# Two feed-forward layers in two phases over all tokens, the gated tiles kept in float32, each half weight tile decoded when it is needed, SBUF laid out by hand

## The chip, the core and the metric

The program runs on one core of one Trainium2 chip. The metric is the device time of one execution in microseconds (us); three executions of the kernel before are known, and one more execution, with the profiler on, gives the trace. TensorE (PE) multiplies; VectorE (DVE), ScalarE (ACT) and GpSimd (POOL) work elementwise; SyncE (SP) issues the transfers.

## The reference, cut to what matters

Clustered attention over 2 batches of 8 heads (768 positions of 64), whose output becomes 1536 tokens of 512, and then two feed-forward layers. Weights arrive as float64.

```
attn = softmax(where(same cluster, scale * q @ k.T, -1e9)) @ v
x = attn.transpose(0, 2, 1, 3).reshape(1536, 512)
h = np.maximum(x @ w_in, 0.0)                                # w_in 512 x 2048
x = (h * h @ w_out).astype(np.float32)                       # w_out 2048 x 512
h = x @ w_in2
g = h * (1.0 / (1.0 + np.exp(-1.702 * h)))
return (g @ w_out2).astype(np.float32)
```

## The kernel before, in words

**Products.** A float32 operand is split into a high part (a cast to float32r) and a low part (what the cast lost, one subtraction); a product is three passes, high by high, low by high, high by low.

**Attention.** Sixteen heads go in eight pairs, as 96 query tiles: `scores` (L470, L473), `peak` on DVE (L479), `exponents` on ACT (L487), transposes (L494) and their copies (L500), then `values` (L510), the ratio transposes (L527) and `whole` (L537), which multiplies by the ratio and writes a quarter of a token chunk `xs`. The order of everything is a table of keys: each piece is put `at` a number that counts query tiles, the list is sorted, and each engine gets its instructions in that order.

**Feed-forward.** There are 4 token chunks of 384 tokens and 16 weight tiles m (128 hidden units each) in a layer. A step is one chunk with one weight tile, 64 steps a layer, chunk by chunk. In a step `hidden` runs 12 products of 128x384 (L597); the gate makes `r` on ACT (L610, and L616 square; in the second layer L612 sigmoid and L618 product on DVE), its high part `gh` by an ACT cast (L622) and its low part `gl` on DVE (L626). LAG = 3 steps later `reduce_out` runs the output products: 12 of 128x384 in the first layer (L645), 9 of 128x512 in the second (L651), which add up in PSUM over all m. `leave` copies a finished chunk out (L660, L662, or L670 with a transfer), and `split_x` splits the next chunk (L172, L173).

**Weights.** A weight tile has a half for `hidden` (w_in) and a half for the output products (w_out). Both halves come in one transfer of 1024 KB, as float64 bit patterns, and each is decoded in seven stages: magnitude on ACT (L136), clamp, shift and two joins on DVE (L139, L143, L147, L151), a cast on ACT (L157) and a subtraction on POOL (L161). All 16 weight tiles of a layer are held in SBUF for its whole length, so all 32 half tiles must have been decoded by the end of its first chunk: NMID = 5 weight tiles are decoded under the attention, the other 11 during the first chunk's 16 steps; all 16 of the second layer's during the first layer's last chunk and the second layer's first.

## Time and profile before

| what | value |
|---|---|
| three timed executions | 849.98, 848.15, 849.47 us, median 849.47 |
| profiled execution, span | 848.9 us; no other own time of it is known |
| busy in it | PE 807.3, DVE 503.6, ACT 444.0, POOL 231.5 us |
| attention's last product, first product of the feed-forward layers | up to 269.66 us, from 269.66 us |
| last product | ends at 845.36 us |

The profiled execution's own time is its span. The median of the timed runs is 0.6 us above it. Busy time is the sum of the durations of an engine's instructions; what an engine waited for is found in the chain of waits, which follows the work that ended last back from the end.

### The profile page before, as it was taken

Reading aid. Unit: us, or ns where it says so; the run is one execution under the profiler, and the core shown is the slowest. Engines: PE = TensorE matmul, PEld = TensorE weight load, DVE = VectorE, ACT = ScalarE, POOL = GpSimd, SP = SyncE. Lnnn points to the kernel's source line nnn. Section 1 sums busy time; section 2 is a strip of 40 time slices with the busy share of each in tenths; the row PEclk is TensorE's granted clock in tenths of the full one; section 3 lists DMA queues with packets and bytes.
Section 4 is the critical chain, followed back from the end, with each engine's and each line's share of the span. In section 5 each row is a group of like instructions: output and inputs, shape, how many; then the busy total and the mean of one; then the engine's idle time right before and its main releaser. Section 6 shows DMA issues by size and latency. Waiting matters only on the chain.

```text
span 848.9 us, 11910 instructions
## 1 busy us (share of the span) xinstructions
PE 807.3 (95%) x4509; PEld 683.5 (81%) x4509; DVE 503.6 (59%) x896; ACT 444.0 (52%) x890; POOL 231.5 (27%) x181
## 2 busy tenths in 40 slices
PE   6899999999999787999999999989879999999998
PEld 3766666666666787899999999979669999999997
DVE  6877777888889999611111228999983233232321
ACT  5787678788776655643443446564443233222221
POOL 5874474485303544300000003333330000000000
PEclk9899999999999989999999999999989999999999
DMA  4232233242131920000000025352111001000000
GB/s 131 75 103 51 71 85 105 73 128 66 29 149 58 390 97 3 1 1 1 1 1 1 1 78 207 141 195 76 52 48 38 1 1 38 0 1 8 31 1 37
DMA packets 13449, 54.60 MB, mean 64 GB/s; under 512 B 2192, under 2 KB 2192, under 8 KB 9296
## 3 DMA queue, kind: packets, MB, share of 16 engines
q1 hardware_dynamic: 13248, 53.45, 18.9%
q8 instruction: 35, 0.57, 0.3%
q10 hardware_dynamic: 144, 0.39, 0.1%
q14 instruction: 22, 0.18, 0.1%
HBM read 43.02 MB, written 3.15 MB: 54 GB/s over the span
## 4 chain that ended last, share of the span: by engine, by line
PE 68%; DVE 21%; issue 3%; ACT 2%; DMA 1%; POOL 1%; DVEq 0%; ACTq 0%
PE ps_h L597 21%; PE ps_y L651 13%; PE ps_y L645 9%; PE ps_p L494 8%; PE ps_v L510 8%; DVE w L147 5%; DVE w L139 4%; DVE w L151 4%; PE ps_s L470 3%; PE ps_s L473 3%; DVE gl L626 2%; DVE w L143 2%; PE ps_aff L333 1%; DVE r L618 1%; DVE unused L479 1%
## 5 line engine op out<-in xcount | busy, mean ns | idle before, releaser
L597 PE MATMUL ps_h<-xhl,w 128*128 128x384 f32 x1536 | 294.0, 339 | 8.4 <-ACT w L157 3.5
L597 PEld LDWEIGHTS ps_h<-xhl,w 128*128 128x128 f32 x1536 | 274.0, 190 | 17.1 <-ACT w L157 4.0
L161 POOL TENSOR_TENSOR w<-w,w 128x512 fp32r<-128x512 f32 x64 | 97.7, 1535 | 289.9 <-ACT w L157 271.9
L626 DVE TENSOR_TENSOR gl<-r,gh 128x384 fp32r<-128x384 f32 x128 | 77.2, 603 | 146.5 <-ACT gh L622 146.5
L645 PE MATMUL ps_y<-gh,w 128*128 128x384 f32 x512 | 131.9, 338 | 0.0
L651 PE MATMUL ps_y<-w,gh 128*128 128x512 f32 x384 | 121.0, 396 | 1.1 <-ACT gh L622 1.1
L494 PEld LDWEIGHTS ps_p<-ident,e 128*128 128x128 f32 x576 | 67.1, 142 | 56.0 <-ACT pt L500 23.3
L645 PE MATMUL ps_y<-gl,w 128*128 128x384 f32 x256 | 87.8, 343 | 14.1 <-DVE gl L626 14.1
L622 ACT CAST gh<-r 128x384 fp32r<-128x384 f32 x128 | 65.7, 514 | 64.9 <-DVE r L618 62.8
L494 PE MATMUL ps_p<-ident,e 128*128 128x128 f32 x576 | 99.2, 283 | 0.1
L479 DVE TENSOR_SCALAR_CACHE_REDUCE unused<-ps_s 128x768 bf16<-128x768 f32 x96 | 91.5, 953 | 11.4 <-PE ps_s L473 7.8
L487 ACT ACTIVATE e<-ps_s,nm 128x768 f32<-128x768 f32 x96 | 86.6, 902 | 21.9 <-DVE unused L479 13.9
L618 DVE TENSOR_TENSOR r<-ps_h,r 128x384 f32<-128x384 f32 x64 | 35.6, 556 | 104.3 <-ACT r L612 104.3
L645 PEld LDWEIGHTS ps_y<-gh,w 128*128 128x128 f32 x512 | 93.8, 191 | 0.3 <-ACT gh L622 0.3
L612 ACT ACTIVATE r<-ps_h 128x384 f32<-128x384 f32 x64 | 31.3, 490 | 103.6 <-PE ps_h L597 103.5
L651 PEld LDWEIGHTS ps_y<-w,gh 128*128 128x128 f32 x384 | 71.9, 190 | 13.7 <-ACT gh L622 1.7
L510 PE MATMUL ps_v<-pt,raw_v 128*64 128x384 f32 x384 | 82.3, 510 | 0.0
L651 PE MATMUL ps_y<-w,gl 128*128 128x512 f32 x192 | 77.0, 401 | 3.2 <-DVE gl L626 3.2
L500 DVE COPY pt<-ps_p 128x384 f32<-128x384 f32 x96 | 52.7, 549 | 34.3 <-PE ps_p L494 33.3
L610 ACT ACTIVATE r<-ps_h 128x384 f32<-128x384 f32 x64 | 31.2, 488 | 77.0 <-PE ps_h L597 77.0
L157 ACT CAST w<-w 128x512 fp32r<-128x512 f32 x64 | 39.6, 618 | 59.5 <-DVE w L151 59.4
L645 PEld LDWEIGHTS ps_y<-gl,w 128*128 128x128 f32 x256 | 48.9, 191 | 16.7 <-DVE gl L626 16.7
(102 smaller groups left out, 981.3 us busy)
## 6 DMA issues: line engine op xcount, KB each, us to landing
words<-in_w_dram SPq DMA_DIRECT2D x32, 1024.0 KB, 5.0
raw_k<-in_k_t_dram SPq DMA_DIRECT2D x8, 384.0 KB, 3.8
q<-x SPq DMA_DIRECT2D x16, 192.0 KB, 2.6
k<-k SPq DMA_DIRECT2D x16, 192.0 KB, 2.6
raw_v<-in_v_dram SPq DMA_DIRECT2D x8, 384.0 KB, 3.3
out_dram<-o SPq DMA_DIRECT2D x12, 256.0 KB, 2.1
raw_q<-in_q_t_dram SPq DMA_DIRECT2D x7, 384.0 KB, 3.5
q<-oht SPq DMA_DIRECT2D x14, 48.0 KB, 2.1
```

The costliest lines, as they stand in the source:

```text
L161: nc.gpsimd.tensor_tensor(out=t[:, 1, :], in0=x[i].bitcast(F32), in1=t[:, 0, :].bitcast(F32), op=ALU.subtract)
L479: nc.vector.tensor_scalar(out=unused, in0=s_t[g][:, :, :HALF], scalar1=-scale, scalar2=None, op0=ALU.mult, op1=ALU.min, accum_out=m_t[g])
L487: nc.scalar.activation(out=p_t[g].rearrange("p (n f) -> p n f", n=2), in_=s_t.pop(g)[:, :, :HALF], func=AF.Exp, bias=m_t.pop(g), scale=sca ...
L494: nc.tensor.transpose(ps[:, a * P:(a + 1) * P], p_t[g][:, t * P:(t + 1) * P], ident)
L500: (nc.vector.tensor_copy if u else nc.scalar.copy)(out=pt_t[n, j][:, u * TH:(u + 1) * TH, i * P:(i + 1) * P], in_=tp_t.pop((g, u))[:, :HAL ...
L510: nc.tensor.matmul(pv_t[n][j * D:(j + 1) * D, :HALF], lhsT=raw[n // 2, "v"][:, j, t, :], rhs=pt_t[n, j][:, t, :], start=(t == 0), stop=(t ...
L597: nc.tensor.matmul(ps[:, :HALF], lhsT=w[:, 0, a, kk * P:(kk + 1) * P], rhs=x[:, b, kk, :], start=(n == 0), stop=(n == 3 * KD - 1))
L618: nc.vector.tensor_tensor(out=t["r"], in0=t["ps"][:, :HALF], in1=t["r"], op=ALU.mult)
L622: nc.scalar.copy(out=t["gh"], in_=t["r"])
L626: nc.vector.tensor_tensor(out=gl, in0=t["r"], in1=t["gh"].bitcast(F32), op=ALU.subtract)
L645: nc.tensor.matmul(ps, lhsT=lh, rhs=rh, start=(m == 0 and e == 0), stop=(m == MF - 1 and e == 2))
L651: nc.tensor.matmul(ps, lhsT=lh, rhs=w[:, 1, a, :], start=(m == 0 and e == 0), stop=(m == MF - 1 and e == 2))
```

## The change

Each layer now runs in two phases over all 1536 tokens. In the hidden phase, 64 units (weight tile m by chunk c, m outermost) of 12 products each fill 16 tiles `g_t[m]` of gated values in float32, which stay in SBUF. In the output phase the chunks go in two groups g of two chunks s; for each m the output products of both chunks follow, in eight (second layer: six) PSUM banks. Just ahead of them `g_high` (ACT) and `g_low` (DVE) split one chunk's gated values into one of three places `ghl`.

w_in and w_out halves are now loaded (512 KB each, 64 transfers) and decoded apart, by a list of `jobs` that gives each half the unit at which its first stage stands, with 0.3 units between its stages and its load 2.7 units ahead. Decoded halves lie in a ring of two (w_in, and a few of w_out) or in places that have come free. Of the half tiles, 3 instead of 10 are decoded under the attention; 21 in the first hidden phase, 16 in the first output phase (8 of them the second layer's), 16 in the second hidden phase, 8 in the second output phase.

SBUF is two arenas of fixed size, one for float32r and one for float32, and every tile of it is a view at a written offset; the tile pools are gone. In PSUM the first eight units of the first layer use the attention's places, and the tile `banks` takes all eight banks at unit 8. `whole` now also splits its quarter of a chunk (a cast on ACT, a subtraction on DVE), and `split_x` and `xs` are gone; the first layer's results are split straight out of PSUM (`leave_high`, `leave_low`). LAST moves the last `values`, ratio and `whole` earlier, and everything is in one list of keys, in which the first four hidden units stand among the last `values`.

```diff
+LAST = dict(
+    values=(5.984, 6.484, 6.984, 7.484, 7.984, 8.484), inverse=4.238, spread=5.0, ratio=6.6, ratio_out=7.1, whole=8.9,
+)
...
-    LAG = 3 # steps from hidden to output products
-    W_EARLY = (51.456, 63.886) # query tiles at which the first weight tiles are decoded
-    W_PITCH = 4.887 # the next weight tiles: query tiles between them
-    W_FIRST = 0.265 # in steps: the rest of the first layer
...
+    KB = 1024
+    ROOM = {F32R: 97 * KB, F32: 110 * KB + 512}
+    arena = {t: arena_p.tile([P, n // 4], t, name=f"arena_{n}") for t, n in ROOM.items()}
...
+    xhl = [view(12 * KB * c, [2, KD, HALF], F32R) for c in range(NC)]
+    slots = [60 * KB + 4 * KB * i for i in range(7)] + [48 * KB + 4 * KB * i for i in range(3)]
+    x_slots = [24 * KB + 4 * KB * i for i in range(6)]
+    ghl = [view(88 * KB + 3 * KB * i, [2, HALF], F32R) for i in range(3)]
+    g_at = [14 * KB + 512 + 6 * KB * m for m in range(MF)]
+    g_t = [view(a, [NC, HALF]) for a in g_at]
+    r_p, tmp, o_p = Places(0, 4608), Places(4608, 4608 + 6 * KB), Places(0, g_at[0])
+    words_at = 10 * KB + 512
+    places = Places(g_at[0], g_at[15])
...
+    def slot_of(layer, which, m):
+        ring = slots[8:] if layer == 0 else slots[:2]
+        rest = slots[:8] if layer == 0 else slots[2:]
+        if which == 0:
+            return rest[7] if layer == 0 and m == 2 else ring[m % 2]
+        return rest[m] if m < 8 else x_slots[m - 8] if m < 14 else ring[m - 14]
...
-            words.append(w_pools[place].tile([P, 2, DM, 2], I32, tag="w", name=f"words{layer}_{m}"))
-            nc.sync.dma_start(out=words[0].rearrange("p i f w -> p i (f w)"), in_=(w1, w2)[layer][m].bitcast(I32))
+            nc.sync.dma_start(out=words.rearrange("p f w -> p (f w)"), in_=(w1, w2)[layer][which, m].bitcast(I32))
...
-    def split_x(i, kk):
-        nc.scalar.copy(out=t[:, 0, kk, :], in_=xs[c][:, kk, :])
-        nc.vector.tensor_tensor(out=t[:, 1, kk, :], in0=xs[c][:, kk, :], in1=t[:, 0, kk, :].bitcast(F32), op=ALU.subtract)
...
             def whole(n):
-                nc.vector.tensor_tensor(out=xs[2 * b + u][:, hp, :], in0=pv_t.pop(n)[:, :HALF], in1=rb_t.pop(n), op=ALU.mult)
+                x, t = rb_t.pop(n), xhl[2 * b + u]
+                nc.vector.tensor_tensor(out=x, in0=pv_t.pop(n)[:, :HALF], in1=x, op=ALU.mult)
+                nc.scalar.copy(out=t[:, 0, hp, :], in_=x)
+                nc.vector.tensor_tensor(out=t[:, 1, hp, :], in0=x, in1=t[:, 0, hp, :].bitcast(F32), op=ALU.subtract)
...
+            H_LEN, Y_LEN = MF * NC, 2 * MF
+            LAYER = H_LEN + 2 * Y_LEN
+            def moment(u):
+                return NG + W_BEGIN + W_UNIT * u
+
+            def open_banks():
+                actx.close()
+                pool = ctx.enter_context(tc.tile_pool(name="psum2", bufs=1, space=bass.MemoryType.PSUM, reuse_waits="tile"))
+                banks.append(pool.tile([P, 8, 512], F32, name="banks"))
+            def hidden(layer, u, m, c):
+                if banks:
+                    ps = bank(u)
+                else:
+                    if u % 2 == 0:
+                        ps_u["two"] = ps_s("ps_h")
+                    ps = ps_u["two"][:, u % 2, :]
+                ps_u[layer, m, c] = ps
...
+            def outer(layer, m, c):
+                r, ps = r_t.pop((layer, m, c)), ps_u.pop((layer, m, c))
+                if layer == 0:
+                    nc.scalar.activation(out=g_t[m][:, c, :], in_=r, func=AF.Square)
+                else:
+                    nc.vector.tensor_tensor(out=g_t[m][:, c, :], in0=ps[:, :HALF], in1=r, op=ALU.mult)
+            def half_of(g, m, s):
+                return ghl[((g * MF + m) * 2 + s) % 3]
+
+            def g_high(g, m, s):
+                nc.scalar.copy(out=half_of(g, m, s)[:, 0, :], in_=g_t[m][:, 2 * g + s, :])
+
+            def g_low(g, m, s):
+                t = half_of(g, m, s)
+                nc.vector.tensor_tensor(out=t[:, 1, :], in0=g_t[m][:, 2 * g + s, :], in1=t[:, 0, :].bitcast(F32), op=ALU.subtract)
...
+            def leave_high(g, i):
+                s, d = divmod(i, KD)
+                nc.scalar.copy(out=xhl[2 * g + s][:, 0, d, :], in_=bank(i)[:, :HALF])
+
+            def leave_low(g, i):
+                s, d = divmod(i, KD)
+                x = xhl[2 * g + s]
+                nc.vector.tensor_tensor(out=x[:, 1, d, :], in0=bank(i)[:, :HALF], in1=x[:, 0, d, :].bitcast(F32), op=ALU.subtract)
...
+            def weights(layer, which, m, first, pitch=0.3):
+                h = first - LAYER * (first >= LAYER)
+                hidden_now = h < H_LEN
+                n = turns[0] = turns[0] + 1
+                place = words_at if n % 2 else g_at[15] if hidden_now else 0
+                load_w, parts = w_stages(layer, which, m, place)
+                at(moment(first - 2.7), load_w)
+                for x, f in enumerate(parts):
+                    at(moment(first + pitch * x), f)
...
+            at(moment(8) - 0.01, open_banks)
+            for layer in range(2):
+                u0 = LAYER * layer
+                y0 = u0 + H_LEN
+                jobs = []
+                for m in range(MF):
+                    if m < 3 and layer == 0:
+                        jobs.append((-14 + 4 * m, 0, m))
+                    elif m < 2:
+                        jobs.append((u0 - Y_LEN + 5 + 4 * m, 0, m))
+                    else:
+                        jobs.append((u0 + 4 * (m - 1), 0, m))
+                for m in range(MF):
+                    if m >= 8:
+                        jobs.append((y0 + 3.6 + 3.2 * (m - 8), 1, m))
+                    elif layer == 0:
+                        jobs.append((u0 + 2.2 + 4 * (1, 3, 5, 7, 8, 10, 11, 12)[m], 1, m))
+                    elif m < 6:
+                        jobs.append((u0 - Y_LEN + 12 + 3.2 * m, 1, m))
+                    else:
+                        jobs.append((u0 + 14.2 + 8 * (m - 6), 1, m))
+                for first, which, m in sorted(jobs):
+                    weights(layer, which, m, first)
+                order = [(m, c) for m in range(MF) for c in range(NC)]
+                if layer == 0:
+                    order[:8] = [(0, 0), (0, 1), (1, 0), (1, 1), (0, 2), (1, 2), (0, 3), (1, 3)]
+                for u, (m, c) in enumerate(order):
+                    at(moment(u0 + u), hidden, layer, u, m, c)
+                    at(moment(u0 + u + 1.05), inner, layer, m, c)
+                    at(moment(u0 + u + 1.35), outer, layer, m, c)
+                for g in range(2):
+                    for m in range(MF):
+                        u = y0 + Y_LEN * g + 2 * m
+                        for s in range(2):
+                            at(moment(u + s - 1.8), g_high, g, m, s)
+                            at(moment(u + s - 1.4), g_low, g, m, s)
+                        for i in range(NT if layer else 8):
+                            at(moment(u + 2.0 * i / (NT if layer else 8)), reduce_out, layer, g, m, i)
...
-        steps = [(i, m) for i in range(2 * NC) for m in range(MF)]
...
-        for m in range(NMID, MF):
-            weights(at, 0, m, m - NMID + W_FIRST, 1.0, m - NMID + W_FIRST - W_AHEAD)
-        for m in range(MF):
-            first = (NC - 1) * MF + LAG + W_FIRST2 + W_PITCH2 * m
-            weights(at, 1, m, first, 1.0, max(first - W_AHEAD2, (NC - 1) * MF + LAG + m + 0.6))
-        for s, (i, m) in enumerate(steps):
-            at(s, hidden, i, m)
-            for o, f in zip(W_GATE2 if i >= NC else W_GATE, gates(i, m)):
-                at(s + o, f)
-            if i + 1 < 2 * NC and MF - 6 <= m < MF - 6 + KD:
...
```

In what order PE comes to the feed-forward layers: before (L510 are the last `values`, the number in a weight's name is its place in the program), and after, where arena_58 is the float32r arena and arena_59 the float32 arena.

```order
L510 MATMUL ps_v<-pt_3077,raw_v 64x384
L510 MATMUL ps_v<-pt_3104,raw_v 64x384
L597 MATMUL ps_h<-xhl,w_0_2180 128x384 [waits DVE_49,PE_49]
L597 MATMUL ps_h<-xhl,w_0_2180 128x384 x11
L597 MATMUL ps_h<-xhl,w_1_2579 128x384 x12
L597 MATMUL ps_h<-xhl,w_2_3110 128x384 x12
L597 MATMUL ps_h<-xhl,w_3_3211 128x384 [waits PE_49,Activation_49]
L597 MATMUL ps_h<-xhl,w_3_3211 128x384 x3
L597 MATMUL ps_h<-xhl,w_3_3211 128x384 [waits Pool_49]
L597 MATMUL ps_h<-xhl,w_3_3211 128x384 x7
L645 MATMUL ps_y_3395<-gh,w_0_2180 128x384 [waits PE_49,Activation_49]
```

```order
L638 MATMUL ps_h<-arena_58 128x384 x12
L638 MATMUL ps_h<-arena_58 128x384 [waits Activation_49]
L638 MATMUL ps_h<-arena_58 128x384 x10
L638 MATMUL ps_h<-arena_58 128x384 [waits DVE_49]
L638 MATMUL ps_h<-arena_58 128x384 x12
L638 MATMUL ps_h<-arena_58 128x384 [waits Activation_49]
L638 MATMUL ps_h<-arena_58 128x384 x10
L638 MATMUL ps_h<-arena_58 128x384 [waits DVE_49]
L638 MATMUL ps_h<-arena_58 128x384 x12
L638 MATMUL banks<-arena_58 128x384 [waits PE_49,Activation_49]
L638 MATMUL banks<-arena_58 128x384 x47
```

Output products no longer follow three steps behind; unit after unit of hidden products stands there, and the ninth unit, the first into `banks`, waits for ACT.

On ACT after, around the relu (L648) of units 5 to 8, the seventh being the last into `ps_h` (L655 square, L185 magnitude, L204 the decoding's cast):

```order
L648 ACTIVATE arena_59<-ps_h 128x384
L185 ACTIVATE arena_59<-arena_59 128x512 [waits DMAHW0_49,Pool_49]
L655 ACTIVATE arena_59<-arena_59 128x384 [waits Activation_49]
L648 ACTIVATE arena_59<-ps_h 128x384 [waits PE_49]
L655 ACTIVATE arena_59<-arena_59 128x384 [waits Activation_49]
L204 CAST arena_58<-arena_59 128x512 [waits DVE_49]
L185 ACTIVATE arena_59<-arena_59 128x512 [waits DMAHW1_49,Pool_49]
L648 ACTIVATE arena_59<-ps_h 128x384
L655 ACTIVATE arena_59<-arena_59 128x384 [waits Activation_49]
L648 ACTIVATE arena_59<-banks 128x384 [waits PE_49]
```

Between the relus of units 5 and 7 stand two magnitudes and a cast that waits for DVE's four stages; units are counted from 0, so the last relu out of `ps_h` is unit 7's.

On DVE, the gate's low parts among the decoding: before, in the first layer's first chunk (`gl` is the gate's low part, w_... a half tile being decoded), and after, where the first output phase begins (L668 is `g_low`, L188 to L200 the four stages).

```order
L139 TENSOR_SCALAR w_3286<-w_3286 128x512 [waits Activation_49]
L143 TENSOR_SCALAR w_3286<-w_3286 128x512 [waits DVE_49]
L626 TENSOR_TENSOR gl<-r,gh 128x384 [waits Activation_49]
L147 SCALAR_TENSOR_TENSOR w_3286<-words_5_3265,w_3286 128x512 [waits DMAHW2_49,DVE_49]
L139 TENSOR_SCALAR w_3311<-w_3311 128x512 [waits Activation_49]
L151 SCALAR_TENSOR_TENSOR w_3286<-words_5_3265,w_3286 128x512 [waits DVE_49]
L143 TENSOR_SCALAR w_3311<-w_3311 128x512 [waits DVE_49]
L147 SCALAR_TENSOR_TENSOR w_3311<-words_5_3265,w_3311 128x512 [waits DVE_49]
L139 TENSOR_SCALAR w_3319<-w_3319 128x512 [waits Activation_49]
L151 SCALAR_TENSOR_TENSOR w_3311<-words_5_3265,w_3311 128x512 [waits DVE_49]
L143 TENSOR_SCALAR w_3319<-w_3319 128x512 [waits DVE_49]
L626 TENSOR_TENSOR gl<-r,gh 128x384 [waits Activation_49]
```

```order
L668 TENSOR_TENSOR arena_58<-arena_59,arena_58 128x384 [waits Activation_49] x3
L668 TENSOR_TENSOR arena_58<-arena_59,arena_58 128x384 [waits PE_49,Activation_49] x3
L188 TENSOR_SCALAR arena_59<-arena_59 128x512 [waits Activation_49]
L192 TENSOR_SCALAR arena_59<-arena_59 128x512 [waits DVE_49]
L196 SCALAR_TENSOR_TENSOR arena_59<-arena_59 128x512 [waits DMAHW5_49,DVE_49]
L668 TENSOR_TENSOR arena_58<-arena_59,arena_58 128x384 [waits PE_49,Activation_49]
L200 SCALAR_TENSOR_TENSOR arena_59<-arena_59 128x512 [waits DVE_49]
L668 TENSOR_TENSOR arena_58<-arena_59,arena_58 128x384 [waits PE_49,Activation_49] x2
L188 TENSOR_SCALAR arena_59<-arena_59 128x512 [waits Activation_49]
L192 TENSOR_SCALAR arena_59<-arena_59 128x512 [waits DVE_49]
L668 TENSOR_TENSOR arena_58<-arena_59,arena_58 128x384 [waits PE_49,Activation_49]
```

Between two `gl` stood eight stages of decoding; between two `g_low` now stand one to three, and `g_low` waits for PE too, which must have left the place it writes.

## Rows read from the trace of the kernel before

**Rows 1.** The page: span, busy time by engine, PE's busy tenths.

```profile
span 848.9 us, 11910 instructions
...
PE 807.3 (95%) x4509; PEld 683.5 (81%) x4509; DVE 503.6 (59%) x896; ACT 444.0 (52%) x890; POOL 231.5 (27%) x181
...
PE   6899999999999787999999999989879999999998
```

**Rows 2.** Windows: length, busy us of PE, PEld, DVE, ACT, POOL, clock, DMA.

```profile
20.00:269.66 249.66, 246.71 (x1572) 161.96 (x1572) 202.84 (x420) 193.74 (x398) 131.92 (x99) 0.98 0.29 80
...
284.00:348.00 64.00, 49.28 (x244) 45.76 (x243) 62.68 (x87) 35.87 (x70) 34.56 (x21) 0.92 0.28 109
348.00:548.00 200.00, 200.00 (x1155) 199.70 (x1154) 68.78 (x112) 94.66 (x189) 15.80 (x11) 1.00 0.11 38
548.00:638.00 90.00, 77.93 (x369) 68.57 (x368) 82.91 (x127) 44.54 (x88) 31.80 (x22) 0.94 0.28 106
```

**Rows 3.** PE's timeline where the feed-forward layers begin: start, length, work.

```profile
269.66 8.59 PE L597 MATMUL ps_h<-xhl,w 128*128 128x384 f32 x48
```

**Rows 4.** The chain that ended last: one step of each layer, the end; start, length.

```profile
433.54 2.08 PE ps_y L645 x12
435.62 2.08 PE ps_h L597 x12
...
832.96 2.08 PE ps_y L651 x9
835.04 2.10 PE ps_h L597 x12
837.14 8.22 PE ps_y L651 x36
```

**Rows 5.** PE's waits from 269.66 us: total, times, longest.

```profile
PE ps_y L645 <- DVE gl L626: 14.1, 8, 3.2
```

**Rows 6.** Timelines of DVE and POOL in the first chunk: start, length.

```profile
301.95 1.83 POOL L161 TENSOR_TENSOR w<-w,w 128x512 fp32r<-128x512 f32 x1 [1.62 <-ACT w L157]
...
302.55 1.51 DVE L139 TENSOR_SCALAR w<-w 128x512 f32<-128x512 f32 x1
...
305.64 1.52 DVE L139 TENSOR_SCALAR w<-w 128x512 f32<-128x512 f32 x1
```

**Rows 7.** DVE's lines by source: ns least, median, most; first and last start.

```profile
L139 DVE TENSOR_SCALAR w<-w x64: 385/420/1525, 162.4 to 628.2; 128x512 f32<-128x512 f32 x64
L143 DVE TENSOR_SCALAR w<-w x64: 397/420/1487, 164.5 to 628.6; 128x512 int32<-128x512 int32 x64
L147 DVE SCALAR_TENSOR_TENSOR w<-words,w x64: 677/689/1789, 168.0 to 629.5; 128x512 int32<-128x512 int32 x64
L151 DVE SCALAR_TENSOR_TENSOR w<-words,w x64: 676/692/1915, 172.3 to 630.2; 128x512 int32<-128x512 int32 x64
L626 DVE TENSOR_TENSOR gl<-r,gh x128: 545/559/1672, 276.6 to 838.9; 128x384 fp32r<-128x384 f32 x128
```

**Rows 8.** Groups by line: busy us, mean ns, idle before.

```profile
L622 ACT CAST gh<-r 128x384 fp32r<-128x384 f32 x128 | 65.7, 514 | 64.9 <-DVE r L618 62.8
L136 ACT ACTIVATE w<-words 128x512 f32<-128x512 f32 x64 | 43.2, 675 | 6.4 <-POOL w L161 3.7 <-DMA words<-in_w_dram 2.7
L157 ACT CAST w<-w 128x512 fp32r<-128x512 f32 x64 | 39.6, 618 | 59.5 <-DVE w L151 59.4
L610 ACT ACTIVATE r<-ps_h 128x384 f32<-128x384 f32 x64 | 31.2, 488 | 77.0 <-PE ps_h L597 77.0
```

**Rows 9.** DMA issues: KB of one, median us to landing.

```profile
words<-in_w_dram SPq DMA_DIRECT2D x32, 1024.0 KB, 5.0
raw_k<-in_k_t_dram SPq DMA_DIRECT2D x8, 384.0 KB, 3.8
```

**Rows 10.** Timelines of ACT and PE in the attention, around one exponential.

```profile
181.58 0.89 ACT L487 ACTIVATE e<-ps_s,nm 128x768 f32<-128x768 f32 x1
...
182.63 0.61 PE L470 MATMUL ps_s<-k,x 128*128 128x384 f32 x2
```

## The forecast

> **What bounds the kernel now.** I read the page first. PE is busy 95% of the span, and its row of busy tenths has two dips, one a little behind the first third and one at the second [rows 1]. So the kernel is bound by PE except in two stretches, and the question is what holds PE there. The windows say it: in 284 to 348 us PE works 49.28 of 64 us and DVE 62.68, in 548 to 638 us PE 77.93 of 90 and DVE 82.91; between them PE works all of 200 us, with DVE at a third [rows 2]. The reader should see that DVE is full exactly where PE is not. The first stretch is the first layer's first chunk, the second the layer change, the two places in which half tiles are decoded. The granted clock, too, falls there, to means of 0.92 and 0.94.
>
> Next, how long the feed-forward layers would take if PE never waited. They begin at 269.66 us [rows 3] and the last product ends at 837.14 + 8.22 = 845.36 us [rows 4], 575.7 us in all. The chain of waits has steps that stand back to back: 2.08 and 2.08 us in the first layer, 2.08 and 2.10 us in the second [rows 4]. That gives 64 x 4.16 + 64 x 4.18 = 533.8 us. So 575.7 - 533.8 = 41.9 us are lost. Of these the first window holds 14.7 us of idle PE and 64 x 0.08 = 5.1 us of clock, the second 12.1 and 90 x 0.06 = 5.4, together 37.3 [rows 2]; 4.6 us lie beside the windows or in the rounding of a step.
>
> Why DVE is full: in the first chunk it decodes 22 half tiles. Two successive clamps start at 302.55 and 305.64 us, so a half tile takes DVE 3.09 us there, of which the clamp alone is 1.51 us, beside a POOL subtraction that began at 301.95 and lasts 1.83 [rows 6]; the clamp's median is 0.42 [rows 7]. With 16 `gl` of 0.56 us the chunk asks DVE for 22 x 3.09 + 9.0 = 77 us, while PE needs 16 x 4.16 = 66.6. PE then stands waiting for `gl`, queued behind the decoding: 14.1 us in 8 waits, the largest sum of any wait in the layers [rows 5].
>
> **The change, part by part.**
>
> *Products.* Their number and shapes stay: 128 units of 12, 64 of 12, 64 of 9. PE's work stays 533.8 us.
>
> *Decoding spread out.* A phase lasts 64 x 2.08 = 133 us of PE's time. With 3.09 us for a half tile, as dear as in the crowded chunk, DVE's work per phase is: first hidden phase 21 x 3.09 = 65 us; first output phase 16 x 3.09 + 64 `g_low` x 0.56 + 16 `leave_low` x 0.56 = 94; second hidden phase 49 + 64 gate products x 0.56 = 85; second output phase 25 + 36 = 61. All lie below 133, so DVE has 39 us or more to spare in each, where it lacked 10 in one chunk. ACT has two gate passes of 0.49 (the relu's price, taken for the square too) and 21 x (0.675 + 0.618) us of decoding in its fullest phase, 90 us [rows 8]. With DVE no longer the bound the 41.9 us go, the clock's 10.5 among them, since the clock fell only in the stretches in which PE stood idle.
>
> *Loads.* 64 transfers of 512 KB stand for 32 of 1024 KB. One takes between 3.8 us (384 KB) and 5.0 us (1024 KB) [rows 9]. The load stands 2.7 units = 5.6 us ahead of its first stage, so 0 us. If that cover were gone (a load held behind the last reading of its place), a decoding would start some us late, and still be ahead of its use by about a unit.
>
> *Attention.* It loses seven half tiles (DVE 7 x 3.09 = 21.6 us, ACT 7 x 1.29 = 9.0) and gains the splits in `whole`, 16 x 0.56 on DVE and 16 x 0.51 on ACT, 9.0 and 8.2 us. The order on PE around the end is otherwise the same, and the four hidden units among the last `values` only change places with them. PE works 246.71 of 249.66 us there [rows 2], so there is nothing to win beyond 2.9 us, and I take 0 both ways. What it could cost is the second rival.
>
> *The hand-over of PSUM (new).* Unit 8 is the first into `banks` and waits for ACT's relu of unit 7, in ACT's order behind unit 5's relu, a magnitude, a cast that waits for DVE's four stages, and another magnitude. From unit 5's end: 0.49 + 0.675 + stages of 0.42 + 0.42 + 0.69 + 0.69 = 2.22 (3.3 if one collides with POOL, by the clamp's 1.51) + 0.618 + 0.675 + 0.49 = 5.2 to 6.3 us [rows 6 to 8]. PE is through units 6 and 7 after 4.16 us. So it waits 1.0 to 2.1 us, once; I take 1.5, between its ends because the magnitude's own POOL partner may or may not be running. Behind the waiting product stand only hidden products.
>
> *Splits just in time (new).* `g_high` of a chunk may start once PE has left the place, three uses back, which is 2 units = 4.16 us ahead of need. Its own chain is 0.51 + 0.56 [rows 7, 8] and some 0.2 of hand-overs, 1.3 us. Up to three decoding stages may stand ahead of `g_low` (0.42 + 0.42 + 0.69 = 1.5) and one magnitude or cast ahead of `g_high` (0.7). The slack is 4.16 - 1.3 - 2.2 = 0.7 us at worst, 2.9 at best. From 0 (all hidden) to the first rival's 26 us; I take 1.0 for 128 uses and the changes of group, near the lower end, because the slack is positive without a collision.
>
> *End.* From the last product to the end of the span 848.9 - 845.36 = 3.5 us [rows 1, 4], the same copy and transfer after.
>
> **Sum.** 269.7 + 533.8 + 1.5 + 1.0 + 3.5 = 809.5 us for a profiled execution, against its own 848.9. The median of the timed runs (849.47) is 0.6 above that span; so **810.0 us**, 4.6% less. What a measurement of this kernel can tell from no change is about 0.2%, 1.7 us.
>
> **The rivals.**
>
> *1. `g_low` is held up by POOL.* `gl` took 0.56 us as a rule and 1.67 at most, 1.1 more [rows 7]. In the output phases 24 half tiles are decoded, each with a POOL subtraction. If each held up one `g_low` with the slack gone, PE would wait 24 x 1.1 = 26 us: 836 us; at half of them 823. For it: the collisions are plain in the trace, the clamp at 1.51 beside POOL against 0.42 [rows 6, 7]. The Trainium skill (SBUF — State Buffer, section "SBUF: two separate sides") says that VectorE and GpSimd share a port pair that one instruction holds for its whole length while the other blocks fully; the trace agrees, with those 1.51 us. Against it: the clamp or a join stands behind a POOL subtraction more often than `g_low` does, and one collision of 1.1 us is more than the worst slack of 0.7 only where three stages stand ahead. Chance 0.13.
>
> *2. The split in `whole` delays the attention.* ACT's cast of 0.51 us waits for DVE and stands ahead of an exponential. Around 181 us the exponential and what follows it end just before the scores that reuse its place: it begins at 181.58, lasts 0.89, and the scores start at 182.63, 0.16 us later [rows 10]. A cast plus its wait of up to 0.56 us is 1.07; 16 of them are 17 us at most: up to 826, likely 812 to 820. Against it: seven half tiles leave, which were as long on the same engines. Chance 0.08.
>
> *3. The other side, slower: DVE stays the bound.* If in the output phases every DVE instruction ran at its longest (1.53 + 1.49 + 1.79 + 1.92 = 6.7 us a half tile, 1.67 a `g_low` [rows 7]), the first output phase would ask 16 x 6.7 + 64 x 1.67 = 214 us, 81 over its 133, and the second 8 x 6.7 + 107 = 161, 28 over: 919 us. The time of before is reached once the two phases together are 39 us over, with the first alone at 172 us of DVE. Against it: POOL, beside which these were seen to lengthen, has in the first output phase only 16 x 1.8 = 29 us of work, and cannot lengthen 80 instructions. Chance 0.04.
>
> *4. The decoding is not spread in effect*, because the two places of the bit patterns hold loads back. In the densest stretch two jobs lie 4 units = 8.3 us apart in one place; a load takes 3.8 to 5.0 us and its reading up to the last join 0.675 + 2.2 to 3.3, together 6.7 to 9.0. At the long end each turn is 0.7 us late, 3.5 us over the five turns of that stretch, of which the unit in hand hides 2.1. For about 849 us, no change, loads would have to be late throughout. Chance 0.02.
>
> **How the numbers follow.** My forecast, 806 to 815: 0.70. Better than 806, if also the attention's 2.9 us come back and nothing new waits: 0.03. The rivals: 0.13, 0.08, 0.04, 0.02. The range runs from 804 to 824: it holds the forecast, nearly all of rival 2 and the lower half of rival 1, and leaves out about 0.15. Faster by over 0.2%: 0.70 + 0.03 + 0.13 + 0.08 = 0.94; the same 0.02; slower 0.04.
>
> **What would show it.** Right: PE's busy tenths without the two dips, the clock at 0.99 or more behind 290 us; the first output phase from about 404 to 537 us; DVE's share in every phase under three quarters; one wait of PE for a relu, 1 to 2 us, near 287 us. Wrong: in the output phases PE waiting for `g_low` beside POOL subtractions (rival 1); PE waiting for exponentials every half pair (rival 2); DVE above 90% in a phase (rival 3). I would be most wrong if a wait of a few tenths stood before each of the 128 uses of `ghl`: 0.2 us each is 26 us.

## The result and the profile after

The changed kernel takes 813.86 us (812.78 to 815.49, four runs) against 848.81 for the kernel before in the same comparison: ratio 0.9586, 95% interval 0.9571 to 0.9602, 4.1% faster. The forecast was 810.0, its range 804 to 824. The profiled execution took 814.13 us with a span of 812.4, so 1.7 us lie around the span.

The page of the changed kernel, the same lines as [rows 1] (span, busy time by engine, PE's busy tenths, and the granted clock's):

```profile
span 812.4 us, 12091 instructions
...
PE 791.9 (97%) x4509; PEld 674.5 (83%) x4509; DVE 473.2 (58%) x890; ACT 441.5 (54%) x880; POOL 216.7 (27%) x181
...
PE   5899999999999989999999999999999999999998
...
PEclk9899999999999999999999999999999999999999
```

Both dips of PE are gone; one small notch is left behind the first third. PE's timeline of the changed kernel (start, length, line, tiles, count, and what PE waited for) shows the hand-over of PSUM and then each phase in one row (the first hidden phase is cut off behind its first seven products). L638 is a hidden product, L676 and L682 the output products of the first and second layer.

```profile
268.71 1.51 PE L553 MATMUL ps_v<-arena 128*64 128x384 f32 x8
...
280.36 10.70 PE L638 MATMUL ps_h<-arena 128*128 128x384 f32 x60
293.65 2.61 PE L638 MATMUL banks<-arena 128*128 128x384 f32 x7 [2.58 <-ACT arena L648]
...
411.60 133.28 PE L676 MATMUL banks<-arena 128*128 128x384 f32 x768
544.72 133.28 PE L638 MATMUL banks<-arena 128*128 128x384 f32 x768
677.84 130.76 PE L682 MATMUL banks<-arena 128*128 128x512 f32 x576
```

From 293.65 us PE never waits again, where it lost 41.9 us before. Windows over the phases (length, busy us of PE, PEld, DVE, ACT, POOL, clock, DMA), the answer to [rows 2]: DVE is at 43 to 59% in each.

```profile
291.07:410.00 118.93, 116.35 (x663) 116.36 (x664) 51.30 (x82) 79.07 (x155) 27.10 (x21) 0.99 0.27 89
410.00:543.00 133.00, 133.00 (x770) 133.00 (x769) 77.91 (x138) 56.90 (x111) 20.61 (x16) 1.00 0.21 68
543.00:676.00 133.00, 133.00 (x769) 133.00 (x769) 71.97 (x133) 52.93 (x102) 20.66 (x16) 1.00 0.18 60
676.00:808.60 132.60, 132.60 (x588) 109.76 (x586) 58.72 (x102) 45.69 (x87) 10.33 (x8) 1.00 0.13 45
```

**Where the forecast's 809.5 us of span and the measured 812.4 part:**

| term | forecast | trace | difference |
|---|---|---|---|
| attention, up to the last half's first value (265.01 us before) | 0 | 268.71 us | +3.7 |
| from there to the end of unit 7 | 21.29 (269.66 - 265.01 + 8 x 2.08) | 22.36 (to 293.65 - 2.58) | +1.1 |
| the hand-over's wait | 1.5 | 2.58 | +1.1 |
| 248 units from unit 8 on, with 1.0 for the splits | 517.2 + 1.0 | 515.0 (293.65 to 808.61) | -3.2 |
| end | 3.5 | 3.8 | +0.3 |

The sum is +3.0 by rounding, for 2.9. The -3.2 are 1.0 for splits that cost nothing and 3.6 for products, less 1.4 of clock (below). Another 0.9 us of the timed 813.86 is what lies around the span, which I had taken as 0.6 from the median.

### The profile page after: what moved, and what is told of

It is laid out like the page before. It is cut to its first block, busy times and chain, and to the rows that moved or that the text cites. A ratio compares the mean times of both kernels' runs of the same rounds, so it can differ in the third digit from the quotient of the medians.

```text
span 812.4 us, 12091 instructions
## 1 busy us (share of the span) xinstructions
PE 791.9 (97%) x4509; PEld 674.5 (83%) x4509; DVE 473.2 (58%) x890; ACT 441.5 (54%) x880; POOL 216.7 (27%) x181
## 4 chain that ended last, share of the span: by engine, by line
PE 86%; DVE 6%; ACT 2%; issue 0%
PE banks L638 31%; PE banks L676 16%; PE banks L682 16%; PE ps_v L553 6%; PE ps_p L537 6%; PE ps_s L513 3%; PE ps_s L516 3%; DVE arena L522 2%; PE ps_h L638 2%; DVE arena L583 2%; ACT arena L530 1%; PE ps_aff L376 1%; DVE arena L543 1%; PE ps_r L570 1%; ACT arena L582 1%; PE ps_back L393 0%
## 5 line engine op out<-in xcount | busy, mean ns | idle before, releaser
L638 PE MATMUL banks<-arena 128*128 128x384 f32 x1440 | 251.4, 335 | 2.6 <-ACT arena L648 2.6
L638 PEld LDWEIGHTS banks<-arena 128*128 128x128 f32 x1440 | 250.9, 189 | 2.9 <-ACT arena L648 2.9
L207 POOL TENSOR_TENSOR arena<-arena,arena 128x512 fp32r<-128x512 f32 x64 | 82.5, 1289 | 414.1 <-ACT arena L204 366.2
L668 DVE TENSOR_TENSOR arena<-arena,arena 128x384 fp32r<-128x384 f32 x128 | 78.4, 612 | 126.4 <-ACT arena L664 125.4
L676 PE MATMUL banks<-arena 128*128 128x384 f32 x768 | 133.3, 334 | 0.0
L676 PEld LDWEIGHTS banks<-arena 128*128 128x128 f32 x768 | 133.1, 188 | 0.0
L682 PE MATMUL banks<-arena 128*128 128x512 f32 x576 | 130.8, 389 | 0.0
L682 PEld LDWEIGHTS banks<-arena 128*128 128x128 f32 x576 | 108.1, 188 | 22.4
L537 PEld LDWEIGHTS ps_p<-arena 128*128 128x128 f32 x576 | 66.5, 141 | 56.4 <-ACT arena L543 23.0
L530 ACT ACTIVATE arena<-ps_s,arena 128x768 f32<-128x768 f32 x96 | 86.5, 901 | 25.9 <-DVE arena L415 11.8
L537 PE MATMUL ps_p<-arena 128*128 128x128 f32 x576 | 98.9, 282 | 0.2
L522 DVE TENSOR_SCALAR_CACHE_REDUCE arena<-ps_s 128x768 bf16<-128x768 f32 x96 | 91.3, 951 | 9.4 <-PE ps_s L516 4.9
L553 PE MATMUL ps_v<-arena 128*64 128x384 f32 x384 | 82.7, 511 | 0.0
L188 DVE TENSOR_SCALAR arena<-arena 128x512 f32<-128x512 f32 x64 | 34.3, 535 | 64.8 <-ACT arena L185 64.5
L513 PE MATMUL ps_s<-arena 128*128 128x384 f32 x192 | 58.4, 385 | 4.1 <-ACT arena L530 3.7
L204 ACT CAST arena<-arena 128x512 fp32r<-128x512 f32 x64 | 39.6, 619 | 35.4 <-DVE arena L200 35.4
```

The costliest lines, as they stand in the source:

```text
L207: nc.gpsimd.tensor_tensor(out=halves[:, 1, :], in0=x[0].bitcast(F32), in1=halves[:, 0, :].bitcast(F32), op=ALU.subtract)
L513: nc.tensor.matmul(ps[:, n, :HALF], lhsT=x_s[i][:, t * P:(t + 1) * P], rhs=k1_s[i][:, n * HALF:(n + 1) * HALF], start=True, stop=False)
L522: nc.vector.tensor_scalar(out=unused, in0=s_t[g][:, :, :HALF], scalar1=-scale, scalar2=None, op0=ALU.mult, op1=ALU.min, accum_out=m_t[g])
L530: nc.scalar.activation(out=p_t[g].rearrange("p (n f) -> p n f", n=2), in_=s_t.pop(g)[:, :, :HALF], func=AF.Exp, bias=m_t.pop(g), scale=sca ...
L537: nc.tensor.transpose(ps[:, a * P:(a + 1) * P], p_t[g][:, t * P:(t + 1) * P], ident)
L553: nc.tensor.matmul(pv_t[n][j * D:(j + 1) * D, :HALF], lhsT=raw[n // 2, "v"][:, j, t, :], rhs=pt_t[n, j][:, t, :], start=(t == 0), stop=(t ...
```

## The experiments

**Is DVE's load in the crowded stretches the lost time?** The kernel before, with the two joins left out:

```diff
-        return load, [magnitude, clamp, shift, join_low, join_high, high, low]
+        return load, [magnitude, clamp, shift, lambda i: None, lambda i: None, high, low]
```

> The kernel before without the two joins of the decoding (the weights keep neither sign nor lowest bits; everything else is done). If the lost 41.9 us come from DVE's load in the two crowded stretches: a half tile takes DVE 0.42 + 0.42 to 1.51 + 0.42 us, so the first chunk asks 22 x 0.84 to 1.93 + 9 = 27 to 51 us of DVE against PE's 66.6, both dips vanish, 807 to 818 us. Rival, the time was in the loads, the layout or the order of the products: at most the waits for the decoding go, 835 us or more.

It took 807.83 us, ratio 0.9505 (0.9489 to 0.9522). The windows of that kernel, the same stretches as the second and fourth of [rows 2]:

```profile
284.00:348.00 64.00, 64.00 (x371) 64.00 (x370) 39.89 (x54) 42.62 (x85) 23.75 (x17) 1.00 0.10 38
...
548.00:638.00 90.00, 90.00 (x454) 81.71 (x453) 43.33 (x72) 36.31 (x72) 17.72 (x13) 1.00 0.09 33
```

PE works through both, at full clock. With old loads, layout and order of products, DVE's relief alone gives 849.71 - 807.83 = 41.9 us, as much as was reckoned lost; the rival falls. That the two agree to a tenth is chance, but the profile says the same: the feed-forward layers last from 266.62 to 800.86 us there, 534.2 us, where 575.7 were measured before and 533.8 reckoned with no wait.

**Does the average over a phase decide, as the forecast reckoned?** The changed kernel, each DVE stage named done twice, or the joins four times:

```diff
-            nc.vector.scalar_tensor_tensor(out=x[0], in0=words[:, :, 0], scalar=29, in1=x[0],
-                                           op0=ALU.logical_shift_right, op1=ALU.bitwise_or)
+            for _ in range(2):
+                nc.vector.scalar_tensor_tensor(out=x[0], in0=words[:, :, 0], scalar=29, in1=x[0],
+                                               op0=ALU.logical_shift_right, op1=ALU.bitwise_or)
```

(likewise the clamp and `join_high`; in the second kernel `range(4)` for the joins)

> The changed kernel with the clamp and both joins of every decoding done twice (same values). A half tile then takes DVE 4.05 us: 85, 110, 101 and 68 us in the four phases of 133. If a phase's average load decides: no new wait there, 0 to +2 us beside the attention's three half tiles. Rival, the place in DVE's queue decides (g_low behind more stages, slack of 0.7 to 2.9 us): 16 + 8 half tiles of the output phases hold up one use each by up to 1.1 us, +10 to +26.

> The changed kernel with the clamp done twice and both joins four times (same values): 6.8 us a half tile on DVE, 143, 154, 145 and 90 us in the four phases of 133. If the average load decides, the first three are over by 10, 21 and 12: +43 us, 857. Rival, place in the queue decides as well: over 870. Rival, DVE's work is hidden anyway: under 830.

They took 862.23 us (ratio 1.0144, 1.0126 to 1.0163) and 1033.78 (1.2165, 1.2145 to 1.2184). The first is above both its numbers. The second is over 870 as the rival had it, but by far, and only in part from its cause: in its trace from 265 us on PE waits 79.0 us for the decoding's cast and 41.4 for `g_low`. With 110 us of DVE work at most in a phase of 133 (110.57 in the trace), the first is 48 us slower than the changed kernel. PE's waits in the first from 265 us on (total, times, longest; its lines stand 3 later, so L207 is the decoding's cast, L671 `g_low`):

```profile
PE banks L641 <- ACT arena L207: 13.8, 9, 3.0
PE banks L641 <- ACT arena L651: 3.8, 1, 3.8
PE banks L641 <- POOL arena L210: 3.4, 8, 0.5
PE banks L679 <- DVE arena L671: 2.7, 4, 0.8
```

Hidden products wait for their own weights, which come too late; `g_low` hardly matters. These waits do not make up the whole price: unit 8 starts 10.6 us later than in the changed kernel (304.24 against 293.65), and behind the waits the granted clock is lower, 0.94 as the mean of 300 to 444.85 us. Its timelines of ACT and DVE around 340 us show why (L185 magnitude, L189 clamp):

```profile
337.98 0.62 ACT L207 CAST arena<-arena 128x512 fp32r<-128x512 f32 x1 [2.45 <-DVE arena L203]
...
338.89 0.65 ACT L185 ACTIVATE arena<-arena 128x512 f32<-128x512 f32 x1
...
344.17 0.62 ACT L207 CAST arena<-arena 128x512 fp32r<-128x512 f32 x1 [3.28 <-DVE arena L203]
344.70 0.66 ACT L185 ACTIVATE arena<-arena 128x512 f32<-128x512 f32 x1
```

```profile
339.57 1.20 DVE L189 TENSOR_SCALAR arena<-arena 128x512 f32<-128x512 f32 x2 [1.63 <-ACT arena L185]
...
345.39 1.52 DVE L189 TENSOR_SCALAR arena<-arena 128x512 f32<-128x512 f32 x2 [1.25 <-ACT arena L185]
```

ACT waits 3.28 us for DVE at the cast, and only behind it, in its own order, makes the next half tile's magnitude, for which DVE then waits 1.25 us. Half tiles pass one at a time, 344.17 - 337.98 = 6.2 us each, where the densest stretch has two jobs to 4 units, 4.16 us each. The average hid this: what counts is the chain of one half tile against the densest stretch.

So the next kernel puts the magnitude ahead of that cast:

```diff
-                at(moment(first + pitch * x), f)
+                at(moment(first + pitch * x - (0.9 if x == 0 and first > 0 else 0.0)), f)
```

> The kernel with the clamp and the joins done twice (862 us), its magnitudes from unit 0 on put 0.9 units earlier, so that in the dense stretches a half tile's magnitude stands ahead of the cast of the half tile before it on ACT. If the price of the doubled stages is the chain of one half tile after another through ACT's queue (magnitude, DVE's stages, cast, and only then the next magnitude: 6.1 us a half tile where 4.2 are wanted), DVE then works without gaps at 4.05 us a half tile and most of the 48 us come back: 815 to 830. Rival, DVE's load itself: still 855 or more.

It took 839.14 us (0.9879, 0.9844 to 0.9913): 23 of the 48 us come back, fewer than expected. The waits for the cast fell from 13.8 to 3.4 us. The timelines of DVE and POOL in that kernel show what then holds (L193 is the shift, L210 POOL's subtraction):

```profile
353.10 0.88 DVE L189 TENSOR_SCALAR arena<-arena 128x512 f32<-128x512 f32 x2
354.02 1.47 DVE L193 TENSOR_SCALAR arena<-arena 128x512 int32<-128x512 int32 x1
...
358.31 0.88 DVE L189 TENSOR_SCALAR arena<-arena 128x512 f32<-128x512 f32 x2
```

```profile
353.92 1.29 POOL L210 TENSOR_TENSOR arena<-arena,arena 128x512 fp32r<-128x512 f32 x1 [3.92 <-ACT arena L207]
```

In the densest stretches DVE now works without a gap, 5.2 us a half tile, because the shift beside POOL's subtraction takes 1.47 us instead of 0.43; my 4.05 had left the collision out. The chain is shown as the first limit. That DVE's rate in the densest stretch is the second is read from this timeline, and no run tests it. Of the 23.8 us of span that are left against the changed kernel, 7.9 stand ahead of unit 8 (301.52 against 293.65), in the attention, whose three half tiles stayed slow.

**How much slack has `g_low`?** A first try with two places for the split tiles instead of three (`ghl` is made with two as well):

```diff
-            def half_of(g, m, s):
-                return ghl[((g * MF + m) * 2 + s) % 3]
+            def half_of(g, m, s):
+                return ghl[s]
```

> The changed kernel with two places for the split gated tiles instead of three: g_high may start 2.08 us ahead of need instead of 4.16. With a chain of 1.3 us and up to 2.2 us of other work ahead, PE comes up to 1.4 us short beside each of the 24 decodings in the output phases, none elsewhere: +5 to +30 us. Rival, the chain has far more slack than worked out: 0.

It took 986.38 us, which says nothing about slack: `g_high` stands 1.8 units ahead, and with two places that is ahead of the last products that read the old values, so these used other values and PE and the splits waited for each other in turn. This is mended by putting `g_high` and `g_low` 1.15 and 0.85 units ahead:

> The changed kernel with two places for the split gated tiles, and g_high and g_low put 1.15 and 0.85 units ahead of use instead of 1.8 and 1.4, so that a place is written behind its last reading. In the changed kernel's trace the low parts are ready 1.98 us ahead of use at least, 3.37 as the median; a place that comes free 2.08 us later leaves -0.1 at least and 1.29 as the median: 0 to +1 us. By the forecast's slack (0.7 us at worst) it would cost up to 1.4 us beside each of 24 decodings: +10 to +30.

It took 814.50 us (0.9586, 0.9559 to 0.9613), no change, as read from the changed kernel's trace: a low part is ready 1.98 us ahead of PE's first use of it at least (the least over 128 of the use's start minus the end of L668).

**What did the attention and the hand-over pay?** Three edits, alone and together. First the relu:

```diff
-                        jobs.append((u0 + 4 * (m - 1), 0, m))
+                        jobs.append((u0 + 4 * (m - 1) + (0.4 if layer == 0 and m == 3 else 0.0), 0, m))
-                        jobs.append((u0 + 2.2 + 4 * (1, 3, 5, 7, 8, 10, 11, 12)[m], 1, m))
+                        jobs.append((u0 + 2.2 + 4 * (1.15, 3, 5, 7, 8, 10, 11, 12)[m], 1, m))
-                    at(moment(u0 + u + 1.35), outer, layer, m, c)
+                    at(moment(u0 + u + (2.1 if layer == 0 and u == 6 else 1.35)), outer, layer, m, c)
```

> The changed kernel with unit 7's relu ahead of the decoding's cast and magnitude, and of unit 6's square, on ACT. In the changed kernel's trace the relu of unit 6 starts only when unit 7 has ended (both lie in one PSUM tile), and five ACT instructions, 2.58 us, follow before unit 8. If that order is the price: two relus remain, 0.49 + 0.48 and some 0.1, so PE waits 1.1 us there, 1.5 us less in the whole. Rival, the forecast's chain from unit 5's end over DVE's stages: the relu waits as long as before, 2.6 us.

It took 811.22 us (0.9545, 0.9528 to 0.9563); the wait is 0.96 us. ACT's timeline of the changed kernel before that unit, where L648 is the relu, L655 the square, L204 the cast, L185 the magnitude:

```profile
291.10 0.49 ACT L648 ACTIVATE arena<-ps_h 128x384 f32<-128x384 f32 x1 [1.71 <-PE ps_h L638]
291.62 0.52 ACT L655 ACTIVATE arena<-arena 128x384 f32<-128x384 f32 x1
292.05 0.60 ACT L204 CAST arena<-arena 128x512 fp32r<-128x512 f32 x1
292.56 0.66 ACT L185 ACTIVATE arena<-arena 128x512 f32<-128x512 f32 x1
293.12 0.48 ACT L648 ACTIVATE arena<-ps_h 128x384 f32<-128x384 f32 x1
```

Unit 6's relu waits until 291.10, when unit 7 has ended: both lie in one PSUM tile. The five instructions are the 2.58 us. The wait had a second price. The windows from unit 8 on, first two of the changed kernel (20 us and, of these, the first 3), then one of this one:

```profile
293.65:313.65 20.00, 20.00 (x107) 20.00 (x108) 8.06 (x14) 11.73 (x23) 4.22 (x4) 0.93 0.25 83
...
293.65:296.65 3.00, 3.00 (x9) 3.00 (x10) 2.44 (x4) 0.50 (x1) 0.35 (x1) 0.50 0.18 72
```

```profile
292.03:312.00 19.97, 19.97 (x115) 19.97 (x116) 9.39 (x16) 13.98 (x28) 5.19 (x4) 1.00 0.31 106
```

Behind 2.58 us without products the clock is 0.93 over 20 us, because it is 0.50, the level of 1.2 GHz, for the first 3: that costs 1.4 us. Behind 0.96 us it is 1.00. The other profiles of this section repeat it: from unit 8 to the first output product PE takes 117.9 to 118.2 us in the four that have a wait of 2.58 or 2.59 us (the changed kernel, the two places put later, and the second and third edit below), and 116.6 us in the three that have 0.96. The span falls from 812.4 to 809.3, 1.6 by the wait and 1.4 by the clock.

Second, the split's subtraction later on DVE:

```diff
-                nc.vector.tensor_tensor(out=t[:, 1, hp, :], in0=x, in1=t[:, 0, hp, :].bitcast(F32), op=ALU.subtract)
+                if n in LATE:
+                    x_low[n] = x, t, hp
+                else:
+                    whole_low(x, t, hp)
...
+                if n in LATE:
+                    at(NT * n + when["whole"] + 0.77, lambda n: whole_low(*x_low.pop(n)), n)
```

> The changed kernel with the low part of the split in whole later on DVE, behind the next peak, for the halves 0, 2, 4, 6, 8, 10, 11, 12. In the changed kernel it lasts 1.75 us beside POOL's subtractions of k in six of these, and scores come 0.34 us later from there on in five. If the collision is the price: 0.56 us there, and the delay of the scores against the kernel before no longer grows by 0.34 a pair nor by 0.5 at tile 82: 2.2 us less. Rival, ACT's cast holds up the exponentials: no change.

Third, the first two casts behind an exponential:

```diff
-                at(moment(first + pitch * x), f)
+                at(moment(first + pitch * x) + (0.3 if first < -8 and x >= 5 else 0.0), f)
```

> The changed kernel with the decoding's cast, for the first two half tiles, behind the exponential that it stood ahead of on ACT. In the changed kernel ACT waits 2.1 and 2.4 us for DVE before these casts, and the scores of tiles 90 and 93 come 0.85 and 1.19 us later from there on. If so, both steps of the delay go: 2.0 us less. Rival, the delay there is DVE's load by the split and the stages: no change.

> The changed kernel with all three edits: if the prices add up, 1.5 + 2.2 + 2.0 us less than the changed kernel, 808.2 us, 0.952 of the kernel before. Rival, PE waits elsewhere for what now comes late: 811 or more.

The second edit took 811.79 us (0.9552, 0.9534 to 0.9569), the third 812.83 (0.9564, 0.9547 to 0.9582), and all together 806.51 (0.9492, 0.9479 to 0.9506). Against the changed kernel's 813.86 the single edits give 2.6, 2.1 and 1.0 us, from two executions each, where 1.5, 2.2 and 2.0 were expected, and the three together 7.4. The start-up differs by up to 2.6 us from profile to profile, so I read the attention's part as the delay of the scores' second products against the kernel before, from tile to tile. Worked out from the timelines, in us:

```
steps in the delay of scores, at tile   17    29    41    53    65    82    90    93   | tiles 4 to 95
changed kernel                          0.35  0.33  0.34  0.33  0.35  0.51  0.85  1.19 |  4.54
split later                             0     0     0     0     0     0     0.86  1.18 |  1.94
casts behind exponentials               0.37  0.35  0.34  0.35  0.34  0.51  0     0    |  2.69
all three                               0     0     0     0     0     0     0     0    |  0.00
```

Each edit takes away its own steps and no other of these. Smaller steps are left out, 0.3 us in sum, and so is one of -0.38 at tile 77 in the kernels with the split later (the second and fourth line), which stays unexplained. What the split ran into, in the changed kernel (by source: ns least, median, most; then DVE and POOL around one of the six long ones, L583 the split, L350 POOL's subtraction of k's low part in two pieces):

```profile
L583 DVE TENSOR_TENSOR arena<-arena,arena x16: 557/559/1770, 56.4 to 281.7; 128x384 fp32r<-128x384 f32 x16
```

```profile
116.60 3.71 POOL L350 TENSOR_TENSOR arena<-arena,arena 64x768 fp32r<-64x768 f32 x2
```

```profile
118.98 1.75 DVE L583 TENSOR_TENSOR arena<-arena,arena 128x384 fp32r<-128x384 f32 x1 [0.58 <-ACT arena L582]
```

It ends at 120.7, a little behind POOL's 120.3, so that the copy, the peak and the exponential behind it come late; moved behind the next peak it takes 0.61 us at most. The Trainium skill (SBUF — State Buffer, section "SBUF: two separate sides") says that of VectorE and GpSimd, sharing a port pair, one blocks fully while the other's instruction lasts; the trace agrees, with 1.75 us for 0.56.

The third step, on ACT and PE of the changed kernel at tile 93 (L204 the decoding's cast, L530 the exponential, L513 scores):

```profile
256.19 0.62 ACT L204 CAST arena<-arena 128x512 fp32r<-128x512 f32 x1 [2.42 <-DVE arena L200]
256.71 0.89 ACT L530 ACTIVATE arena<-ps_s,arena 128x768 f32<-128x768 f32 x1
```

```profile
257.75 0.62 PE L513 MATMUL ps_s<-arena 128*128 128x384 f32 x2 [0.92 <-ACT arena L530]
```

ACT stands 2.42 us at a cast that waits for DVE, with an exponential queued behind it, and PE waits for that. All three together are 1.7 us under the 808.2 that was expected; the clock's 1.4 were not in that sum.

**Does the mixing of values and hidden products cost?** All three edits, and the last values ahead of unit 0:

```diff
-    values=(5.984, 6.484, 6.984, 7.484, 7.984, 8.484), inverse=4.238, spread=5.0, ratio=6.6, ratio_out=7.1, whole=8.9,
+    values=(5.984, 6.08, 6.16, 6.24, 6.32, 6.4), inverse=4.238, spread=5.0, ratio=6.3, ratio_out=6.6, whole=7.1,
```

> The kernel with all three edits (806.5 us) and the last half's values all ahead of the first hidden unit instead of among the first four. In the changed kernel the stretch from the last half's first value to the end of unit 7 takes PE 22.36 us, and the same instructions 21.29 by the rows of the kernel before. If the seven changes of shape between values and hidden products cost the 1.07 us: 21.3 to 21.5 us in the trace. Rival, it is the products of units 3 to 7 (10.70 us for five) whatever stands between: 22.3.

It took 805.46 us, ratio 0.9475 (0.946 to 0.9491), the lowest of all, though not apart in time from the kernel before it, whose profiled span is even the shorter (803.8 us for 804.3). In PE's timeline the stretch goes from 264.36 to 269.01 + 16.94 = 285.95 us, 21.59, where the changed kernel and the one with all three edits took 22.36: 0.8 of the 1.1 us are the mixing's, 0.3 stay open.

```profile
264.36 2.80 PE L553 MATMUL ps_v<-arena 128*64 128x384 f32 x16
...
269.01 16.94 PE L648 MATMUL ps_h<-arena 128*128 128x384 f32 x96
```

## Why the prediction was right, and where its steps were off

*The bound and the gain.* Right, and shown: relieving DVE alone gives the kernel before 42 us, and the changed kernel has no wait from unit 8 to the end and a full clock from 313.65 us on (1.00 as the mean from there to the last product).

*Decoding spread out.* The outcome was right and the reckoning was not. "All lie below 133" is no test: with 110 us in a phase the kernel is slower than before. The changed kernel decodes a half tile in 4.2 and 4.3 us from one cast to the next (349.38 - 345.15 and 353.67 - 349.38, the ends of three casts), 4.16 wanted in its densest stretch: there it has only what `jobs` put ahead, and the w_in halves from the fourth on (but for the second layer's first two) are cast 3.2 to 4.6 us before their use.

*Attention.* The term that was most mis-sized: 0 for 3.7 us, and for 4.54 of steps from tile 4 to 95, since in its profile the changed kernel had reached tile 4 1.15 us earlier than the kernel before, within the spread of the start-up, which is luck. I weighed what leaves against what comes, engine by engine. But the seven half tiles leave other places than those in which the splits come. Rival 2 had the place and a size in its range (up to 17 us), with half its mechanism: ACT's cast of the split cost nothing, the DVE subtraction beside POOL cost 1.7 (five steps of 0.34), the plain split at tile 82 0.5, and the casts of decoding 2.0.

*The hand-over.* 1.5 for 2.58 + 1.4 of clock. The chain from unit 5's end over DVE's stages was not what came last: DVE was through at 291.34 us. The relu of unit 6 waited for unit 7, as the shared PSUM tile would have told.

*Splits just in time.* 1.0 for 0. The slack was not 0.7 us at worst. Beside decoding it was 2.25 at least, even with three or four stages between two `g_low`, for most of them ran while DVE would have waited for `g_high` (125.4 us of such waits stay in the trace). The least of all, 1.98 us, is at 478.05 us, where the groups change and `leave_low` stands between two `g_low`, which the forecast had not priced. Rival 1's collisions came, ten `g_low` of 128 took over 0.7 us, 1.34 at most, all inside the slack.

*Products.* 3.6 us too much, which hid part of the rest: that the span came out within 2.9 us is partly luck. The range was not luck, for without this and the 1.0 of the splits the terms that were too low would have made about 817 us of span. I took a step of the second layer at 2.08 + 2.10 us, products of 512 columns between products of 384. In phases of one shape a unit takes 133.28 / 64 = 2.08 and 130.76 / 64 = 2.04 us. The row of the kernel before that had it, 36 products in 8.22 us [rows 4], gives 2.055 for nine.

Rival 3 would have been far likelier than 0.04 with the decoding twice as long, and its deciding point of 39 us was much too far off. Rival 4, the turn of a half tile, was nearest to the true limit, though it is ACT's order that sets the turn and not the places of the bit patterns.

## What to carry to other kernels

Work that is made just in time is bounded by its chain through in-order queues, so compare the time of one piece from start to start with the densest stretch, not the engine's sum with the phase. A wait that one engine makes at another's result holds everything queued behind it: put the first stage of the next piece ahead of the last stage of this one, and nothing urgent behind a cast that waits. When a change moves small instructions into a tuned stretch, look for what runs on POOL at that moment and for what stands next on DVE and ACT, rather than adding up busy time.

## What the runs showed of the hardware that was not expected

A DVE subtraction of 128x384 took 1.75 us for 0.56 beside POOL's subtractions, and a shift of one input 1.47 for 0.43. A wait of 2.58 us in a stream of products was followed by a granted clock of 0.50 for 3 us, one of 0.96 us by 1.00. Nine products of 512 columns took 2.04 us among their own kind, and with twelve of 384 in turn the pair took 4.18 for 4.12.
